# Routing the first batch in four parts instead of two, with one load and the first expert block moved in the order of issue

## The chip, the cores and the metric

The kernel runs on one core of a Trainium2 chip. The metric is the device time of one execution in microseconds (us). The engines are TensorE (PE, matmuls; PEld is its weight load), VectorE (DVE), ScalarE (ACT), GpSimd (POOL) and SyncE (SP), which here only issues DMAs. Each engine works through its own instructions in order; they wait for each other by semaphores.

## What is computed

The reference takes x of shape 8 x 2496 x 256 in float32, replaces it by the real part of its two-dimensional Fourier transform, and sends the 19968 rows through a mixture of 8 experts, each row through one:

```
X = np.fft.fft(np.fft.fft(x, axis=1), axis=2).real      # 8 x 2496 x 256
x = X.reshape(19968, 256)
logits = x @ w_gate                                     # 19968 x 8
expert_idx = np.argmax(logits, axis=1)
gate_w = softmax(logits)[arange, expert_idx]
for e in range(8):
    rows = expert_idx == e
    y[rows] = np.maximum(x[rows] @ w1[e], 0) @ w2[e]     # 256 -> 1024 -> 256
out = gate_w[:, None] * y
```

## The kernel before

A batch is one of the 8 sequences. Its way has these stages.

- **first(b)** (L325): loads x of the batch in three thirds (`load`, L284, 896 KB each, buffers of `xq`: three), folds each third on DVE (`fold`, L299; the folds' instructions are L306, L295, L296, L297), does the first step of the transform along the sequence on PE (`half1`, L311, tile `s`), copies it out on ACT (L321) and writes it to a scratch tensor Td in HBM (L342). For b of 1 and more it also issues the loads of batch b + 1.
- **regroup(b, h)** (L351): two DMAs on SP's queue that read Td back in another layout (tiles `t4`).
- **second(b)** (L361): in `group` (L374) the second step of the transform (tile `p2`, copied to `zz` at L379); then, for 2 halves of HW = 5 columns each, one column at a time: matmuls into `p3`, ACT's copies L405 and L408, DVE's pair of L410 that writes the rows, and ACT's `mirror` (L384). A column gives two slots of 128 rows, a half ten slots. PSUM tiles of all these come from one pool of three buffers.
- **route(b, h, rows, lg)** (L416): called once at the end of each half; 17 DVE instructions (L424 to L455), one exponential on ACT (L436) and eleven small matmuls (`rk`) that count rows by expert. They find each row's expert, gate and place in the sorted tensor Xs. `base`, the count so far, is handed from one call to the next. At its end the ten slots stand in the queue `waiting`.
- **send** (L462): takes one slot from `waiting` and issues its scatter on POOL, an indirect DMA of 128 rows to Xs (L236). For batch 0 the places are integers already; for later batches ACT and POOL convert them first (L468, L469).
- **plan(b, ...)** (L478): DVE instructions on one partition, which from `base` fix the blocks of rows that can be computed by now, and their expert. It has four yields; batch 0 has two plans, one for blocks of 256 rows (two blocks) and one for blocks of 128 rows (four).
- **experts(todo)** (L730): for each block SP reads the plan's table, loads the expert's weights (L546, L548, 1 MB each) and the block's rows (L536, L540) from Xs, `turn` transposes them on DVE (L584), then come the two matrix products (`ph`, `py`), and POOL scatters the result to the output. SP's load of the first rows waits for all scatters of its batch.

The order of all this on the engines is the order in which the Python program issues it: every stage is a generator, and a main loop (L997) takes a step of `experts` and, by a running account (`due`), so many steps of `side`, which holds the transforms and the routing of later batches. At the start (L967 on) `first(0)` runs through; then x of batch 1 and the two regroup issues of batch 0 go out; seven steps of `early` (which is `first(1)` and its regroup) are taken, and while `second(0)` runs, every second step of it is followed by one of `early`, and every step by a `send`. Then the expert generator starts: until the first plan's table is there it yields (L778), it fetches weights and rows, and then it yields nine more times (L784) before its first `turn`, so that steps of `side` come ahead of the first transposes in DVE's order and of the first `ph` in PE's. For b = 1, `side` weaves the plans of batch 0 with the rest of `early` and then the transforms of batch 1, one step of each by turns:

```
if b == 1:
    side = woven(chain(close(0), through(0)), chain(early, side))
```

The parts of the source that the change touches follow, with the line numbers that the profile uses.

Of the kernel before, what the change touches and what calls it, by code (L numbers as in the profile page):

```python
# [12 lines left out]
F32 = mybir.dt.float32  # L13
BF16 = mybir.dt.bfloat16
I32 = mybir.dt.int32
ALU = mybir.AluOpType
# [34 lines left out]
def bc(ap, axis, n):  # L51
    shape = list(ap.shape)
    shape.insert(axis, n)
    return ap[tuple([slice(None)] * axis + [None])].to_broadcast(shape)
# [127 lines left out]

TICKS = 32
LATE = 4
SHARE, EARLY, ROOM = 0.6, 0.7, 1.2
AHEAD = 12
WARM = 16
# [28 lines left out]
def kernel(ctx: ExitStack, tc, x, w_gate, w1, w2, out):  # L216
# [3 lines left out]
    def mm(o, lhsT, rhs, start=True, stop=True, **kw):  # L220
        nc.tensor.matmul(o, lhsT=lhsT, rhs=rhs, start=start, stop=stop, **kw)  # L221
# [62 lines left out]
    def load(b, q):  # L284

        if b < B:
            xq = xp.tile([NP, 8, D], F32, tag="xq", name="xq", bufs=3)
            row = (b * NQ + q) * NA
            nc.sync.dma_start(out=xq[:].rearrange("p j d -> p (j d)"), in_=x[row:row + NP])
            ahead[b, q] = xq[0:NA]  # L290
# [70 lines left out]
    def second(b):  # L361

        t4 = None

        def turn_last(h):

            nonlocal t4
            t4 = ahead.pop((b, "t4", h))
            n = min(HALF, NG - h * HALF)
            pr = pm_.tile([GP, HALF], F32, tag="m", name="pr")  # L370
            mm(pr[:, 0:n], con["rot"][:], t4[0:GP, 0:n, H])
            act.copy(t4[0:GP, 0:n, H], pr[:, 0:n])  # L372
# [13 lines left out]

        turn_last(0)
        yield
        group(0)
        yield  # L390
        group(1)
        yield
        for h in range(2):
            rows = sp.tile([128, NSL, W], F32, tag="rows", name="rows")
            lg = sp.tile([128, NSL, E], F32, tag="lg", name="lg")
            for i in range(HW):
                w, k = HW * h + i, 2 * i
                if w + 2 < NG:
                    group(w + 2)
                p3 = pm_.tile([128, 2 * NY + 2 * E + 1], F32, tag="m", name="p3")  # L400
                z = zz[:, :, 128 * w:128 * (w + 1)]
                mm(p3[:, 0:NY + 2 * E], z[:, 0], con["rd"][:, 0, 0:NY + 2 * E], True, False, skip_group_check=True)
                mm(p3[:, NY:], z[:, 1], con["rd"][:, 1], False, True, skip_group_check=True)
                zs = sp.tile([128, NY + 1], F32, tag="zs", name="zs")
                act.copy(zs[:], p3[:, NY + 2 * E:])  # L405
                if i:
                    mirror(rows, k - 2)
                act.copy(lg[:, k:k + 2], p3[:, NY:NY + 2 * E].rearrange("p (m e) -> p m e", m=2))  # L408
                for m, op in enumerate((ALU.add, ALU.subtract)):
                    vec.scalar_tensor_tensor(rows[:, k + m, 0:NY], p3[:, 0:NY], zs[:, 0:1], zs[:, 1:],  # L410
                                             op0=ALU.add, op1=op)
                yield
            mirror(rows, k)
            yield from route(b, h, rows, lg)

    def route(b, h, rows, lg):  # L416

        nonlocal base

        def small(name, *dims, dt=F32):  # L420
            return sp.tile([128, *dims], dt, tag=name, name=name)

        mx, eq, v = small("mx", NSL), small("eq", NSL, E), small("v", NSL)
        vec.reduce_max(mx[:], lg[:], axis=AX_X)  # L424
        vec.tensor_tensor(eq[:], lg[:], bc(mx[:], 2, E), op=ALU.is_equal)
        vec.tensor_tensor(eq[:], eq[:], bc(con["rev"][:], 1, NSL), op=ALU.mult)
        vec.reduce_max(v[:], eq[:], axis=AX_X)
        vec.tensor_tensor(v[:], v[:], con["good"][:, h], op=ALU.mult)
        oh = small("oh", NSL + 1, E, dt=BF16)
        vec.memset(oh[:, NSL], 0.0)  # L430
        vec.tensor_tensor(oh[:, 0:NSL], bc(con["rev"][:], 1, NSL), bc(v[:], 2, E), op=ALU.is_equal)
        yield

        su = small("su", NSL)
        vec.tensor_tensor(lg[:], lg[:], bc(mx[:], 2, E), op=ALU.subtract)
        act.activation(lg[:], lg[:], ACTF.Exp)  # L436
        vec.tensor_scalar(rows[:, :, D], con["row"][:, h], float(b * S), None, op0=ALU.add)
        yield

        rk = pm_.tile([128, NSL + 1, E], F32, tag="m", name="rk")  # L440
        mm(rk[:], tri[:], oh[:], True, False)
        for s in range(NSL):
            mm(rk[:, s + 1:], ones[:], bc(oh[:, s], 1, NSL - s), False, s == NSL - 1)
        vec.reduce_sum(su[:], lg[:], axis=AX_X)
        vec.tensor_scalar(su[:], su[:], 1e-9, None, op0=ALU.add)
        vec.reciprocal(rows[:, :, D + 1], su[:])
        yield

        pos, pf, pi = small("pos", NSL, E), small("pf", NSL), small("pi", NSL, dt=I32)
        vec.tensor_tensor(pos[:], rk[:, 0:NSL], bc(base[:], 1, NSL), op=ALU.add)  # L450
        vec.tensor_tensor(pos[:], pos[:], oh[:, 0:NSL], op=ALU.mult)
        vec.reduce_sum(pf[:], pos[:], axis=AX_X)
        vec.tensor_tensor(pf[:] if b else pi[:], pf[:], con["far"][:, h], op=ALU.add)
        nxt = cp.tile([128, E], F32, tag="base", name="base", bufs=2)
        vec.tensor_tensor(nxt[:], rk[:, NSL], base[:], op=ALU.add)  # L455
        base = nxt
        for s in range(NSL):
            waiting.append((b, pf[:, s:s + 1], pi[:, s:s + 1], rows[:, s]))

    waiting = deque()  # L460
# [269 lines left out]
    def experts(todo):  # L730
# [44 lines left out]
        for k, (b, size, last, at) in enumerate(todo):  # L775
            n, m = size // 128, BIG // size
            if not k:
                while todo[0][:3] not in tabs:  # L778
                    yield 0, False
                fetch_some(0, 1)  # L780
                while b not in whole:
                    yield 0, True
                fetch_some(0)
                for _ in range(9):  # L784
                    yield 0, False
                for xT in turn(b, size, xbs[0][0]):
                    pass
# [178 lines left out]
    todo = in_order()  # L966
    for _ in first(0):  # L967
        pass
    load(1, 0)
    load(1, 1)  # L970
    regroup(0, 0)
    regroup(0, 1)
    load(1, 2)
    nc.sync.dma_start(out=bt[:], in_=const_dram("blocks", cv))
    sent(unordered(nc.sync.dma_start(
        out=Xs[E * CAP:].rearrange("(k p) w -> p k w", k=BLK // 128), in_=bc(pad[:], 1, BLK // 128)), "xs"), 0)
# [20 lines left out]
    for b in range(1, B):  # L997

        done, due, room = 0, 0.0, 0.0
        side = chain(steps[b], islice(steps.get(b + 1, iter(())), AHEAD))  # L1000
        ticks = TICKS + AHEAD * (b == 1)
        if b == 1:
            side = woven(chain(close(0), through(0)), chain(early, side))
        blocks = [(size, k * size / BIG, halved(b - 1, size)) for size, k, _ in rounds()[b - 1]]
        total = sum(k * (15 if seven_ else 16) for _, k, seven_ in blocks)
        open_ = sum(k * (8 if seven_ else 16) for _, k, seven_ in blocks)
        while done < total:
            w, full = next(work)
# [72 lines left out]
```

## Time and profile before

| | us |
|---|---|
| eight executions: median (lowest to highest) | 1260.08 (1258.13 to 1261.27) |
| the profiled execution | 1256.42 |
| its span in the profile | 1254.6 |
| PE busy in the span | 1207.7 |
| DVE, POOL, ACT busy | 759.9, 447.3, 430.8 |
| mean clock granted to TensorE | 0.977 of full speed |

The page of the profile starts with each engine's busy time, its share of the span and its number of instructions. Below it the span is cut into 40 equal slices; a digit is the busy share of the slice in tenths, and the line PEclk is the clock that the throttle granted to TensorE, in tenths of full speed. A table of stretches has, for each stretch of time, its length, the busy time and the number of instructions of PE, PEld, DVE, ACT and POOL, then the granted clock, the share of time in which the DMA engines worked, and what they moved in GB/s. A line of the timeline has the start of a group of instructions, their busy time, the engine (SPq and ACTq are the issue of DMAs), the line of the kernel, the operation, what it writes and reads, and how many; in brackets stands how long the engine was idle just before, and what ended that.

### The profile page before, as it was taken

How to read it: one execution, taken by the hardware profiler on the slowest of the kernel's cores; microseconds unless marked ns; L12 is line 12 of the kernel's file. 1: busy time of each engine (PE TensorE's matmuls, PEld its weight loads, DVE VectorE, ACT ScalarE, POOL GpSimd, SP SyncE). 2: the span in 40 equal slices, each digit the busy share in tenths (PEclk: the TensorE clock that was granted, in tenths of full speed). 3: DMA queues.
4: the chain of work that ended last, by engine and by line, in shares of the span. 5: the costliest groups of instructions: out<-in, count | busy, mean ns of one | idle time of the engine just before them, and what ended most of it. 6: DMA issues, size and time to landing. Idle time of an engine off the chain costs nothing.

```text
span 1254.6 us, 22295 instructions
## 1 busy us (share of the span) xinstructions
PE 1207.7 (96%) x7289; PEld 1076.6 (86%) x7289; DVE 759.9 (61%) x1804; ACT 430.8 (34%) x1167; POOL 447.3 (36%) x527
## 2 busy tenths in 40 slices
PE   6759999999999999999999999999999999999997
PEld 4648988777788899888988899889999999999996
DVE  4546334333456788566865578686888884444663
ACT  1424333333244333434243433432333332222222
POOL 0245437064117421471226613472364241111112
PEclk6879999999999999999999999999999999999998
DMA  8859899873649434673336435453347238888887
GB/s 239 270 191 342 308 314 307 227 238 120 146 159 264 140 124 146 197 227 112 102 129 210 136 103 167 133 173 101 110 135 196 103 106 284 281 283 284 280 292 284
DMA packets 163216, 249.79 MB, mean 199 GB/s; under 512 B 118601, under 2 KB 130227, under 8 KB 143516
## 3 DMA queue, kind: packets, MB, share of 16 engines
q1 hardware_dynamic: 146327, 203.28, 51.7%
q0 software_dynamic: 15888, 42.14, 9.2%
q10 hardware_dynamic: 885, 2.94, 0.7%
q8 instruction: 59, 0.97, 0.3%
q14 instruction: 57, 0.47, 0.1%
HBM read 194.91 MB, written 54.83 MB: 199 GB/s over the span
## 4 chain that ended last, share of the span: by engine, by line
PE 82%; DVE 10%; DMA 3%; ACT 2%; issue 2%; POOL 0%; SPq 0%; POOLq 0%; DVEq 0%; ACTq 0%
PE py L221 25%; PE ph L221 13%; PE a L221 11%; PE c L221 9%; PE b L221 6%; PE p L221 6%; PE d L221 5%; PE e L221 4%; PE s L221 3%; DMA xq<-in_x_dram 1%; DVE xT L584 1%; DMA Td<-t 1%; DVE y L684 1%; DVE hT L636 1%; DVE hT L639 1%
## 5 line engine op out<-in xcount | busy, mean ns | idle before, releaser
L236 POOL DMA_INDIRECT out_dram<-y,ro x163 | 161.2, 989 | 625.6 <-ACT y L680 301.5
L221 PE MATMUL py<-w_sb,hT 128*128 128x256 f32 x1504 | 339.5, 380 | 0.0
L221 PEld LDWEIGHTS py<-w_sb,hT 128*128 128x128 f32 x1504 | 281.7, 190 | 36.5 <-issue 1.0
L236 POOL DMA_INDIRECT Xs<-rows,pi x160 | 162.4, 1015 | 110.0 <-DVE rows L410 54.8
L221 PE MATMUL ph<-xT,w_sb 128*128 128x128 f32 (+2 forms) x992 | 170.9, 328 | 11.1 <-DVE xT L584 11.0
L221 PEld LDWEIGHTS ph<-xT,w_sb 128*128 128x128 f32 x992 | 136.3, 193 | 35.1 <-issue 16.7
L410 DVE SCALAR_TENSOR_TENSOR rows<-p,zs 128x129 f32<-128x129 f32 x160 | 48.8, 348 | 128.6 <-ACT lg L408 124.6
L221 PE MATMUL a<-xT,w_sb 128*128 128x256 f32 (+1 forms) x512 | 117.8, 357 | 0.0
L838 DVE TENSOR_SCALAR hT<-ph 128x512 f32<-128x512 f32 x43 | 29.7, 691 | 123.7 <-PE ph L221 63.6
L587 ACT ACTIVATE xT<-xT 128x256 f32<-128x256 f32 (+1 forms) x94 | 36.5, 388 | 180.0 <-DVE xT L584 141.6
L221 PEld LDWEIGHTS a<-xT,w_sb 128*128 128x128 f32 x512 | 88.7, 191 | 9.7 <-DVE xT L584 0.2
L892 ACT ACTIVATE y<-py,xb 128x256 f32<-128x256 f32 x94 | 44.5, 473 | 151.5 <-PE py L221 150.4
L636 DVE TENSOR_TENSOR hT<-hT,b 128x512 f32<-128x512 f32 x57 | 39.2, 688 | 74.8 <-PE b L221 49.3
L646 ACT ACTIVATE hT<-a 128x512 f32<-128x512 f32 x57 | 34.0, 597 | 134.2 <-PE a L221 131.1
L221 PE MATMUL s<-xq,w 104*112 104x256 f32 (+2 forms) x208 | 62.6, 425 | 13.4 <-DVE xq L297 10.9
L469 POOL CAST pi<-due 128x1 int32<-128x1 f32 x140 | 45.1, 322 | 65.2 <-ACT due L468 65.2
L221 PE MATMUL a<-w_sb,hT 128*128 128x128 f32 x528 | 66.0, 276 | 0.0
L221 PEld LDWEIGHTS a<-w_sb,hT 128*128 128x128 f32 x528 | 63.1, 192 | 0.7
L221 PEld LDWEIGHTS p<-table,t 120*128 120x128 f32 x352 | 53.0, 200 | 10.7 <-ACT t L372 2.8
L221 PE MATMUL c<-xT,ws 128*128 128x256 f32 (+1 forms) x256 | 60.3, 363 | 1.0 <-DVE hT L642 0.2
L584 DVE STREAM_TRANSPOSE xT<-xb 128x512 f32<-128x512 f32 (+1 forms) x91 | 56.3, 631 | 7.6 <-DMA xb<-Xs 7.6
L221 PE MATMUL b<-xs,ws 128*128 128x256 f32 (+1 forms) x256 | 58.8, 357 | 0.0
(149 smaller groups left out, 2052.8 us busy)
## 6 DMA issues: line engine op xcount, KB each, us to landing
w_sb<-in_moe_w_dram SPq DMA_DIRECT2D x132, 1024.0 KB
xq<-in_x_dram SPq DMA_DIRECT2D x24, 896.0 KB
xb<-Xs SPq DMA_DIRECT2D x112, 128.0 KB
Td<-t SPq DMA_DIRECT2D x18, 448.0 KB
t<-Td SPq DMA_DIRECT2D x8, 768.0 KB
t<-Td SPq DMA_DIRECT2D x8, 640.0 KB
xb<-Xs SPq DMA_DIRECT2D x52, 64.0 KB
xb<-Xs SPq DMA_DIRECT2D x88, 32.0 KB
```

The lines of the kernel that those rows point to most:

```text
L221: nc.tensor.matmul(o, lhsT=lhsT, rhs=rhs, start=start, stop=stop, **kw)
L236: return unordered(pool.indirect_dma_start(out=dst, out_offset=bass.IndirectOffsetOnAxis(ap=idx, axis=0), in_=rows, in_offset=None, bounds ...
L410: vec.scalar_tensor_tensor(rows[:, k + m, 0:NY], p3[:, 0:NY], zs[:, 0:1], zs[:, 1:], op0=ALU.add, op1=op)
L469: pool.tensor_copy(idx, due[:])
L584: vec.transpose(free(xT[:], 256 * h, [32, n // 32], [BIG, 2], [1, 32]), free(xb, 512 * h, [64, n // 32], [1, 2], [2, 32]))
L587: act.activation(odd, odd, ACTF.Copy, scale=-1.0)
L636: vec.tensor_tensor(h12, h11, b[:], op=add)
L639: vec.tensor_tensor(h21, h12, d[:], op=add)
L646: act.activation(h11, a[:], ACTF.Relu)
L684: vec.tensor_tensor(o, o, p[:], op=add)
L838: vec.tensor_scalar(o, ph[:], 0.0, None, op0=ALU.max)
L892: act.activation(y[:, i % 2], py[:], ACTF.Copy, scale=meta[:, i, 1:2])
```

## The change

It has four parts.

1. `second` calls `route` for batch 0 four times, behind the second, fifth, eighth and tenth column (PARTS: two and three columns in the first half, three and two in the second), with the slots of those columns alone: 4, 6, 6 and 4 slots. Batches 1 to 7 keep two calls. `route` takes a slice of slots; its small tiles are cut to it, and the tiles of places `pf` and `pi` get four buffers. The memset of `oh` moves one instruction ahead, and the mirror of a part's last column is issued at its end.
2. The load of batch 1's third third of x is issued on SP ahead of the two regroup issues of batch 0 instead of behind them.
3. The expert generator yields twelve times and not nine ahead of the first turn.
4. For b = 1 five steps of the plans of batch 0 are taken alone, before the rest of the plans is woven with the transforms of batch 1.

In the order of the built program, four groups of `rk` matmuls (5, 7, 7 and 5) take the place of two of eleven. The first plan and half of the second stand on DVE ahead of the fold of batch 2's first third, where they were mixed with it. The two last `half1` of batch 1 stand behind the second and third column of batch 0 and no longer behind the fourth and fifth. Ahead of the first `ph` on PE stand three columns of batch 1, where there were four. The diff, cut to its core:

```
+PARTS = ((2, 3), (3, 2))
...
         for h in range(2):
...
+            ends = list(np.cumsum(PARTS[h] if not b else (HW,)))
+            lo = 0
             for i in range(HW):
...
-                if i:
+                if i and i not in ends:
                     mirror(rows, k - 2)
...
                 yield
-            mirror(rows, k)
-            yield from route(b, h, rows, lg)
+                if i + 1 in ends:
+                    mirror(rows, k)
+                    yield from route(b, h, rows, lg, slice(lo, k + 2))
+                    lo = k + 2
 
-    def route(b, h, rows, lg):
+    def route(b, h, rows, lg, at):
...
+        n = at.stop - at.start
+        rows, lg = rows[:, at], lg[:, at]
+        mx, v, su = (small(name, NSL)[:, 0:n] for name in ("mx", "v", "su"))
+        eq, pos = (small(name, NSL, E)[:, 0:n] for name in ("eq", "pos"))
+        pf = sp.tile([128, NSL], F32, tag="pf", name="pf", bufs=4)[:, 0:n]
+        pi = sp.tile([128, NSL], I32, tag="pi", name="pi", bufs=4)[:, 0:n]
+        oh = small("oh", NSL + 1, E, dt=BF16)[:, 0:n + 1]
...
-        for s in range(NSL):
-            mm(rk[:, s + 1:], ones[:], bc(oh[:, s], 1, NSL - s), False, s == NSL - 1)
+        for s in range(n):
+            mm(rk[:, s + 1:], ones[:], bc(oh[:, s], 1, n - s), False, s == n - 1)
...
-        for s in range(NSL):
+        for s in range(n):
             waiting.append((b, pf[:, s:s + 1], pi[:, s:s + 1], rows[:, s]))
...
-                for _ in range(9):
+                for _ in range(12):
                     yield 0, False
                 for xT in turn(b, size, xbs[0][0]):
...
-    load(1, 0)
-    load(1, 1)
+    for q in range(NQ):
+        load(1, q)
     regroup(0, 0)
     regroup(0, 1)
-    load(1, 2)
...
         if b == 1:
-            side = woven(chain(close(0), through(0)), chain(early, side))
+            plans = close(0)
+            side = chain(islice(plans, 5), woven(chain(plans, through(0)), chain(early, side)))
```

More of the change, by code (lines that the diff above doesn't have):

```diff
@@ L421, in small @@
             return sp.tile([128, *dims], dt, tag=name, name=name)
[L423 to L429, printed above, removed]
@@ L430, in route @@
-        vec.memset(oh[:, NSL], 0.0)
-        vec.tensor_tensor(oh[:, 0:NSL], bc(con["rev"][:], 1, NSL), bc(v[:], 2, E), op=ALU.is_equal)
+        n = at.stop - at.start
[4 more added lines that the diff above has]
+        pi = sp.tile([128, NSL], I32, tag="pi", name="pi", bufs=4)[:, 0:n]
@@ L432, in route @@
+        oh = small("oh", NSL + 1, E, dt=BF16)[:, 0:n + 1]
+        vec.reduce_max(mx, lg, axis=AX_X)
+        vec.tensor_tensor(eq, lg, bc(mx, 2, E), op=ALU.is_equal)
+        vec.tensor_tensor(eq, eq, bc(con["rev"][:], 1, n), op=ALU.mult)
+        vec.reduce_max(v, eq, axis=AX_X)
+        vec.tensor_tensor(v, v, con["good"][:, h, at], op=ALU.mult)
+        vec.memset(oh[:, n], 0.0)
+        vec.tensor_tensor(oh[:, 0:n], bc(con["rev"][:], 1, n), bc(v, 2, E), op=ALU.is_equal)
         yield
-        su = small("su", NSL)
@@ L435, in route @@
-        vec.tensor_tensor(lg[:], lg[:], bc(mx[:], 2, E), op=ALU.subtract)
-        act.activation(lg[:], lg[:], ACTF.Exp)
-        vec.tensor_scalar(rows[:, :, D], con["row"][:, h], float(b * S), None, op0=ALU.add)
+        vec.tensor_tensor(lg, lg, bc(mx, 2, E), op=ALU.subtract)
+        act.activation(lg, lg, ACTF.Exp)
+        vec.tensor_scalar(rows[:, :, D], con["row"][:, h, at], float(b * S), None, op0=ALU.add)
         yield
-        rk = pm_.tile([128, NSL + 1, E], F32, tag="m", name="rk")
@@ L441, in route @@
-        mm(rk[:], tri[:], oh[:], True, False)
-        for s in range(NSL):
-            mm(rk[:, s + 1:], ones[:], bc(oh[:, s], 1, NSL - s), False, s == NSL - 1)
-        vec.reduce_sum(su[:], lg[:], axis=AX_X)
-        vec.tensor_scalar(su[:], su[:], 1e-9, None, op0=ALU.add)
-        vec.reciprocal(rows[:, :, D + 1], su[:])
-        yield
-        pos, pf, pi = small("pos", NSL, E), small("pf", NSL), small("pi", NSL, dt=I32)
-        vec.tensor_tensor(pos[:], rk[:, 0:NSL], bc(base[:], 1, NSL), op=ALU.add)
@@ L451, in route @@
-        vec.tensor_tensor(pos[:], pos[:], oh[:, 0:NSL], op=ALU.mult)
-        vec.reduce_sum(pf[:], pos[:], axis=AX_X)
-        vec.tensor_tensor(pf[:] if b else pi[:], pf[:], con["far"][:, h], op=ALU.add)
+        rk = pm_.tile([128, NSL + 1, E], F32, tag="m", name="rk")[:, 0:n + 1]
+        mm(rk, tri[:], oh, True, False)
+        for s in range(n):
+            mm(rk[:, s + 1:], ones[:], bc(oh[:, s], 1, n - s), False, s == n - 1)
+        vec.reduce_sum(su, lg, axis=AX_X)
+        vec.tensor_scalar(su, su, 1e-9, None, op0=ALU.add)
@@ L454, in route @@
+        vec.reciprocal(rows[:, :, D + 1], su)
+        yield
+        vec.tensor_tensor(pos, rk[:, 0:n], bc(base[:], 1, n), op=ALU.add)
+        vec.tensor_tensor(pos, pos, oh[:, 0:n], op=ALU.mult)
+        vec.reduce_sum(pf, pos, axis=AX_X)
+        vec.tensor_tensor(pf if b else pi, pf, con["far"][:, h, at], op=ALU.add)
         nxt = cp.tile([128, E], F32, tag="base", name="base", bufs=2)
-        vec.tensor_tensor(nxt[:], rk[:, NSL], base[:], op=ALU.add)
+        vec.tensor_tensor(nxt[:], rk[:, n], base[:], op=ALU.add)
```

## The prediction, made before the changed kernel was run

> **What bounds the kernel now.** I read the page first, then the stretches, then the timeline of the first 100 us; every number below is from these views of the kernel before, except where I say "worked out".
>
> On the page the engine line of TensorE (PE) comes first, then its row of slices:
>
> ```profile
> PE 1207.7 (96%) x7289; PEld 1076.6 (86%) x7289; DVE 759.9 (61%) x1804; ACT 430.8 (34%) x1167; POOL 447.3 (36%) x527
> PE   6759999999999999999999999999999999999997
> PEclk6879999999999999999999999999999999999998
> ```
>
> PE is full from the fourth slice to the last. So the end is: the moment at which PE becomes full, plus the PE work that is left then. The table of stretches gives that moment:
>
> ```profile
> 62.00:76.50 14.50, 10.98 (x52) 9.17 (x52) 12.20 (x56) 5.00 (x18) 11.45 (x11) 0.73 0.74 261
> 76.50:87.50 11.00, 0.00 (x0) 0.00 (x0) 2.71 (x8) 0.66 (x4) 3.89 (x4) 0.67 0.37 104
> 87.50:110.00 22.50, 21.65 (x123) 19.02 (x124) 9.78 (x36) 10.05 (x37) 4.85 (x9) 0.93 0.92 305
> ```
>
> From 76.5 to 87.5 PE does nothing; after it PE is busy 21.65 of 22.5 us, and so on to the end. Who ends the hole is in the timeline:
>
> ```profile
> 53.24 1.11 POOL L236 DMA_INDIRECT Xs<-rows,pi  x1 [52.79 <-DVE rows L410]
> 54.65 0.97 POOL L236 DMA_INDIRECT Xs<-rows,pi  x1 [0.30 <-issue]
> ...
> 63.65 1.89 POOL L236 DMA_INDIRECT Xs<-rows,pi  x1 [0.30 <-issue]
> ...
> 80.33 0.97 POOL L236 DMA_INDIRECT Xs<-rows,pi  x1 [0.30 <-issue]
> 82.93 1.92 SPq L536 DMA_DIRECT2D xb<-Xs  x4
> 86.74 0.71 DVE L584 STREAM_TRANSPOSE xT<-xb 128x512 f32<-128x512 f32 x1 [7.56 <-DMA xb<-Xs]
> 87.50 3.42 PE L221 MATMUL ph<-xT,w_sb 128*128 128x256 f32 x8 [11.04 <-DVE xT L584]
> ```
>
> The first block needs all 20 scatters of batch 0. POOL issues them in one unbroken row, 53.24 to 80.33, 1.28 us apart; then come landing, fetch, transpose. So the path is: routing of the first half, 20 scatters, turn. The change acts on its head.
>
> **Part by part** (lines are those of before; columns of batch 0 are counted from 0).
>
> *The load moved forward* (L973). One SP issue passes the two regroup issues; no instruction is added. Before, it was issued at 30.16 and VectorE (DVE) stood on it until 39.10; the fold behind it ended just as the first L410 could start, 41.85, though lg was there at 41.19. Gain at most 0.7. Loss: its 0.92 MB now run beside the third write of Td0 (25.71 to 29.05), for which regroup waits. DMA moved 356, 260 and 18 GB/s in the stretches 24-26, 26-28, 28-30; the empty last stretch takes some 0.65 MB, the rest costs 0.8 us at 350 GB/s; with no room at all 2.7 us. I take 0 (0.7 against 0.8), bounds -0.7 and +2.7.
>
> *Four routes for two.* A ten-slot route takes DVE from 48.75 (L424) to 52.39 (L455), 3.64 us, 17 instructions that wait for each other. A narrower one has the same 17; its wide ones fall from 0.24 (128x80) towards 0.17 (the 1x32 row), so some 3.3. Two more routes are 6.6 us of DVE ahead of everything later on DVE. On PE the extra rk matmuls (11 take 0.47) are nothing; on ACT two 0.27 exps. The wait added: ACT's exp stands before the copies of the next column, so ACT idles in each route.
> - Column 1's L410 ends at 43.6. Route 1: 43.5 to 46.9. POOL started 1.1 after L453 (52.14 to 53.24), so here at 47.7, 5.5 earlier; four scatters, free at 52.9.
> - Columns 2 to 4 took 44.15 to 48.83, 4.7 us, with the two half1 copies between them. Behind route 1 (ACT and PE run ahead at most by the three buffers of PSUM) they end at 51.9. Route 2: to 55.2, its scatters ready at 56.0. **POOL stands still from 52.9 to 56.0.**
> - Columns 5 to 7 and route 3: 61.7, ready 62.6, ahead of POOL (56.0 + 6 x 1.28 = 63.7). Columns 8, 9 and route 4: 66.7, ready 67.6, ahead of 71.4.
> - Last scatter: 56.0 + 15 x 1.28 = 75.2. Four scatters of before are longer than 0.97 (63.65: 1.89, 65.84: 1.26, 71.24: 1.64, 78.30: 1.72), each beside a fold of x (L306, L295, L296) on DVE. Two folds fall on the last scatters again: I add the first three excesses, 1.9. **77.1 instead of 80.33**; bounds 75.2 and 77.8.
>
> Here a page speaks against the change. The Trainium skill, SBUF — State Buffer, section "SBUF: two separate sides", says that VectorE and GpSimd share a port pair as a lock and that the loser is blocked for the whole instruction. By that a fold's 1.21 + 0.67 + 0.67 could hold scatters for 5.1 us in two folds, the last scatter would start at 80.3 and the sum below would come out near 1262. The trace agrees in part only: the scatter at 67.41 took 0.97 beside the fold at 67.53.
>
> *From the last scatter to the turn.* 80.33 to 87.50 is 7.17. The last scatter landed in 2.35; the median of the 20 is 4.6. Before, the weights (2 MB) were issued at 68.17 and DMA was full until 78, so the last scatter found it empty. Now the plan ends later: route 4 at 66.7, then 20 plan instructions, 1.41 + 0.43 + 1.36 in their three groups, at 70.0; weights until some 80. I add 0.55 of the possible 2.25, as they are nearly through: first ph at 77.1 + 7.17 + 0.55 = **84.8** (84.3 to 86.5).
>
> *Plans first, twelve steps.* In the built program five plan steps now stand ahead of the folds of batch 2, and one column fewer of batch 1 stands ahead of the first ph. On DVE, worked out: ten more plan instructions to 72.0, fold to 75.0, rest of the plan and second fold to 78.9, then three L410 pairs behind matmuls that start on the half clock (s at 66.42: 2.02 for four): the third ends at 83.65. The transpose stands behind it, so ph could start at 84.4. This hides behind the scatters by 0.4 us only; each later us of DVE would then count in full.
>
> *The sum at the turn.* Turn: 84.8 - 87.50 = -2.7. The column deferred behind it (p, pr, p) is 0.94 + 0.13 at full clock: +1.1. **The clock:** the granted clock fell to 0.5 at 59.75 and 80.25, 3.2 and 3.8 us after the last matmul, and came back at 91, so the first ph took 3.42 instead of 1.89 (91.71). With PE at work until 82.3 by the DVE count and the turn at 84.8 the gap is 2.5: -1.5 (0 if cold). Behind the turn DVE has the small fold (L295 to L306, 1.6 us) that was done before it; rk may wait: +0.3 (0 to 1.6). Weights, x and Td2 move with the turn: 0. Sum -2.7 + 1.1 - 1.5 + 0.3 = **-2.8**.
>
> The profiled execution took 1256.42 (span 1254.6 and 1.8 around it): 1253.6. The median of the eight runs is 1260.08, 3.66 above; I carry the difference over: **1257.3 us**. Measurement tells about 0.2%, 2.5 us, from no change.
>
> **Rivals.**
> - *Full gain* (0.25). Routes overlap better, two more cost 4.6 and not 6.6, and POOL hardly stands still: scatters from 47.7 back to back end at 47.7 + 19 x 1.28 + 1.9 = 73.9; DVE is then the bound at 82.4. -5.1 + 1.1 - 1.5 = -5.5: 1254.6. For it: 0.54 us of DVE idle per column. Against: ACT is held by the exp.
> - *The gain is eaten at the turn* (0.15). The last scatter lands in 4.6, ph at 86.5, PE has gone cold: -1.0 + 1.1 + 0.3 = +0.4: 1260.5. For it: the weights come later. Against: DMA is empty at 78 to 80.
> - *The clock falls in the routes* (0.15), the slower case. PE's gaps in the routes are 2.4 to 2.9 by my times; one of 3.4 halves the clock, and the thin work of columns does not lift it (62 to 70 stayed at 0.5 for 3.5 us of steady work). Then p and p take 1.75 and not 0.95 in seven columns: DVE is 5.6 late, ph at 90.0. +2.5 + 1.1 + 0.3 = +3.9: 1264. It decides from a gap of 3.4 us, and makes it slower once the transpose starts after 86.
> - That the change doesn't do what it says is excluded by the built order: four rk groups, the scatters of the first four slots behind the first.
>
> **How the numbers follow.** The forecast has 0.45. With errors of 0.5 to 1 us in several terms, two thirds of it lie beyond 2.5 us: faster 0.30 + 0.25 = 0.55; same 0.15 + 0.15 = 0.30; slower 0.15. The range takes in the full gain and the eaten one with the bounds of the load and of the deferred fold around them, and leaves out most of the clock case: 1253.8 to 1261.6.
>
> **What would show it.** Right: first scatter near 47.7; a hole on POOL of some 3 us after the fourth; last scatter near 77; weights issued near 70.5; first ph near 85 with eight matmuls in 1.9. Wrong: no hole (full gain), a granted clock of 0.5 between 50 and 66 (clock case), a first L410 after 43 (the load), a transpose that waits for DVE's own queue and not for xb (DVE has become the bound).

## The result, and the profile after

| | before | after |
|---|---|---|
| executions: median (lowest to highest), us | 1259.95 (1257.02 to 1262.36) | 1266.42 (1263.66 to 1269.43) |
| the profiled execution, us | 1256.42 | 1264.91 |
| its span, us | 1254.6 | 1263.1 |
| VectorE (DVE) busy, us | 759.9 | 765.1 |

The changed kernel is slower: 1.0054 times the time before, 95% interval 1.0045 to 1.0063. The forecast was 1257.3, the upper end of the range 1261.6.

One caution for all that follows. The profiled execution of before lies 3.5 us below the median of its kernel; those of the other kernels on the quicker chips (see the experiments) lie within 3 us of theirs, on either side. So a difference between two traces tells where time goes, and the ratios tell how much.

On the page of after, the slices of TensorE (PE) and its granted clock:

```profile
PE   5659999999999999999999999999999999999997
...
PEclk9769999999999999999999999999999999999998
```

PE is full from the fourth slice on, as before. Most of the loss is made ahead of that. The stretches, with the columns of the table of before:

```profile
62.00:76.50 14.50, 6.00 (x36) 5.26 (x34) 10.55 (x64) 4.09 (x16) 10.72 (x12) 0.61 0.64 205
76.50:87.50 11.00, 6.74 (x28) 6.00 (x28) 8.57 (x29) 2.96 (x10) 4.15 (x3) 0.58 0.73 237
87.50:110.00 22.50, 18.19 (x99) 15.48 (x100) 11.11 (x39) 8.21 (x30) 1.43 (x4) 0.92 0.79 245
```

Before, PE worked 10.98 us in the first of these, nothing in the second and 21.65 in the third. Now work has spread into the hole (6.74 between 76.5 and 87.5), at a clock of 0.58, and the third stretch is no longer full. The timeline of POOL shows the 20 scatters:

```profile
51.51 1.11 POOL L237 DMA_INDIRECT Xs<-rows,pi  x1 [51.06 <-ACT lg L411]
...
59.71 0.97 POOL L237 DMA_INDIRECT Xs<-rows,pi  x1 [3.27 <-DVE rows L413]
...
77.77 2.07 POOL L237 DMA_INDIRECT Xs<-rows,pi  x1 [0.30 <-issue]
80.14 1.12 POOL L237 DMA_INDIRECT Xs<-rows,pi  x1 [0.30 <-issue]
```

and that of SP's queue the weights of the first block, then its rows, which wait for the last scatter's landing:

```profile
76.44 0.37 SPq L554 DMA_DIRECT2D w_sb<-in_moe_w_dram  x1
...
87.44 1.92 SPq L544 DMA_DIRECT2D xb<-Xs  x4
```

The first scatter starts 1.7 us sooner than before (forecast 5.5), the hole behind the fourth is there as forecast (3.27 us), and the last scatter starts at 80.14, where it stood before. Then 7.30 us pass until the rows can be fetched; before it was 2.60. The first ph follows at 92.10 instead of 87.50.

### The profile page after: what moved, and what is told of

It is laid out like the page before. It is cut to its first block, busy times and chain, and to the rows that moved or that the text cites. A ratio compares the mean times of both kernels' runs of the same rounds, so it can differ in the third digit from the quotient of the medians.

```text
span 1263.1 us, 22338 instructions
## 1 busy us (share of the span) xinstructions
PE 1211.0 (96%) x7291; PEld 1079.2 (85%) x7291; DVE 765.1 (61%) x1838; ACT 431.8 (34%) x1169; POOL 445.1 (35%) x527
## 4 chain that ended last, share of the span: by engine, by line
PE 83%; DVE 9%; DMA 3%; ACT 2%; issue 2%; POOL 1%; SPq 0%; POOLq 0%; DVEq 0%; ACTq 0%
PE py L222 24%; PE ph L222 12%; PE a L222 11%; PE c L222 10%; PE p L222 6%; PE b L222 6%; PE d L222 5%; PE e L222 4%; PE s L222 3%; DMA Td<-t 1%; DVE xT L592 1%; DVE y L692 1%; DMA xq<-in_x_dram 1%; DMA Xs<-rows,pi 1%; DVE hT L644 0%
## 5 line engine op out<-in xcount | busy, mean ns | idle before, releaser
L237 POOL DMA_INDIRECT Xs<-rows,pi x160 | 159.7, 998 | 111.5 <-ACT lg L411 51.8
L413 DVE SCALAR_TENSOR_TENSOR rows<-p,zs 128x129 f32<-128x129 f32 x160 | 48.8, 348 | 143.5 <-ACT lg L411 138.8
L222 PEld LDWEIGHTS s<-xq,w 104*112 104x112 f32 x208 | 38.1, 203 | 29.7 <-issue 11.2
L222 PE MATMUL p<-table,t 120*128 120x120 f32 (+1 forms) x352 | 58.7, 293 | 2.0 <-ACT t L373 2.0
```

The source lines that it names most:

```text
L237: return unordered(pool.indirect_dma_start(out=dst, out_offset=bass.IndirectOffsetOnAxis(ap=idx, axis=0), in_=rows, in_offset=None, bounds ...
```

## The experiments

Eighteen runs of twelve kernels stand in five groups, each group beside before on one chip. In three groups before took 1259.1 to 1260.1, as in the first result; two fell on other chips, where before took 1273.3 and 1274.6. There ACT and DVE stand still in three to five places, for 0.4 to 6.4 us. One of ACT's lines in load_back:

```profile
68.81 0.27 ACT L408 COPY zs<-p 128x130 f32<-128x130 f32 x1 [3.95 <-remote]
```

The bracket says that ACT was idle for 3.95 us and that nothing on this core released it. No trace of the quicker chips has such a line, and I did not find the cause. The intervals of those two groups are about twice as wide, so the verdicts rest on the others; the labels are marked "slower chip".

| label | what it is | ratio to before | interval |
|---|---|---|---|
| after_again | the changed kernel | 1.0044 | 1.0026 to 1.0062 |
| load_back_again | after, load put back | 1.0022 | 1.0010 to 1.0033 |
| load_alone_again | before, load moved | 1.0011 | 0.9999 to 1.0023 |
| w2_behind | after, load put back, second weight matrix behind the rows | 1.0006 | 0.9993 to 1.0019 |
| order_alone_third | before, twelve steps, five plan steps alone | 1.0019 | 1.0009 to 1.0030 |
| routes_alone_again | before, four routes | 1.0006 | 0.9997 to 1.0015 |
| routes_w2_12_again | four routes, twelve steps, second matrix behind | 1.0015 | 1.0005 to 1.0024 |
| w_behind | the same, both matrices behind | 1.0017 | 1.0008 to 1.0026 |
| w_behind_9 | the same with nine steps | 1.0002 | 0.9992 to 1.0011 |
| three_routes | before, three routes | 1.0014 | 1.0004 to 1.0023 |
| load_back | slower chip | 0.9991 | 0.9972 to 1.0011 |
| load_alone | slower chip | 1.0012 | 0.9985 to 1.0040 |
| routes_alone | slower chip | 1.0021 | 1.0001 to 1.0042 |
| order_alone | slower chip | 1.0016 | 0.9995 to 1.0038 |
| order_alone_again | slower chip | 1.0007 | 0.9988 to 1.0026 |
| before_w2_behind | slower chip | 0.9989 | 0.9971 to 1.0007 |
| routes_w2 | slower chip, four routes, second matrix behind | 0.9991 | 0.9972 to 1.0009 |
| routes_w2_12 | slower chip, as routes_w2_12_again | 0.9975 | 0.9960 to 0.9991 |

My theory after the result (theory 1): the moved load delays a write to Td and all that hangs on it. The rival (theory 2): the loss is made at the turn, by the order there and by weights that stand beside the last scatter's landing.

### The load

```diff
-    for q in range(NQ):
-        load(1, q)
+    load(1, 0)
+    load(1, 1)
     regroup(0, 0)
     regroup(0, 1)
+    load(1, 2)
```

load_back is after with this edit; load_alone is before with its reverse. First on a slower chip:

> The changed kernel with the load of batch 1's last third back behind the two regroup issues; the rest of the change stays. Theory 1 (the load): beside it the third write of Td0 landed at 32.95 and not at 29.05, and everything behind regroup is 3.9 us late. Then regroup is issued near 29, the first scatter comes near 47.7, the turn near 88, and the time falls by some 4 us from 1266.4 to about 1262.5. Theory 2 (the order at the turn: plans first, weights beside the last scatters, which lands 7.05 us after its issue where it was 2.35): the late regroup is absorbed by the waits behind it, and the time stays within 1 us of 1266.4.

> The kernel before with nothing changed but the load in front of the regroup issues. Theory 1: regroup near 33, first scatter near 57, turn near 91.4, 1264 us. Theory 2: no more than 1 us above 1260.

Measured: 0.9991 and 1.0012, neither of which tells one theory from the other there. The marks in the trace were as theory 1 has them: regroup issued at 29.49 with the load put back, at 32.56 with the load alone moved. Then again, beside after itself, on a quicker chip:

> The changed kernel itself, unaltered, as the standard for the three runs beside it. Both theories expect a ratio of 1.0045 to 1.0063 against before, as in the first result, and on this chip or any other the same marks in the trace: regroup of batch 0 issued about 33.0, last scatter begun about 80.1 and landed about 7 us later, first rows issued about 87.4.

> The changed kernel with the last third of batch 1's x put back behind the two regroup issues, once more, beside the changed kernel itself. Theory 1 (the moved load delays the write to the scratch tensor, and with it everything up to the turn): regroup issued at 29.0 to 29.5 instead of 33.0, first scatter about 48, routes done about 3.5 us sooner than in the changed kernel, ratio against before 1.000 to 1.003, which is 0.002 to 0.005 below the changed kernel. Theory 2 (the loss is made at the turn, where 2 MB of weights stand in front of the last scatter's packets): the first rows are issued no sooner than 87 us, and the ratio stays at 1.004 or more.

> The kernel before with nothing but the load moved ahead of the regroup issues. Theory 1: regroup issued about 3.5 us later, first scatter 2 to 3.5 us later than in before, last scatter up to 3 us later (POOL's 20 scatters are bound there by their own 1.28 us each), ratio 1.002 to 1.004. Theory 2: ratio within 1.001, since the order at the turn is that of before.

Measured: 1.0044, 1.0022, 1.0011. (In after_again the last scatter began at 81.81 and the rows were issued at 88.88, 1.7 and 1.5 us later than expected; that goes with the clock, below.) In the trace of after, the issues of the load, of the third write to Td (ACT's queue) and of the two regroup reads:

```profile
24.90 0.31 SPq L290 DMA_DIRECT2D xq<-in_x_dram  x1
...
26.80 0.31 ACTq L343 DMA_DIRECT2D Td<-t  x1
...
32.95 0.99 SPq L355 DMA_DIRECT2D t<-Td  x2
```

The same write and reads in load_back_again:

```profile
26.26 0.31 ACTq L343 DMA_DIRECT2D Td<-t  x1
...
29.92 0.99 SPq L355 DMA_DIRECT2D t<-Td  x2
```

From the issue of the write to that of the reads, which wait for its landing, it is 6.15 us with the load beside it and 3.66 without (3.34 before; 6.65 in load_alone_again). The DMA engines in after while the write is under way (PE busy, clock, DMA share, GB/s):

```profile
28.00:30.00 2.00, 0.13 (x1) 0.50 1.02 268
30.00:32.00 2.00, 2.00 (x5) 0.50 0.75 272
32.00:34.00 2.00, 1.63 (x4) 0.50 0.01 4
```

They are full until 30 and empty from 32: the write does not land until the load has nearly gone through. So the load costs 0.0022 of after's 0.0044 when taken out of it (the intervals overlap a little; that of the first result, from 1.0045, lies above), and 0.0011 when put into before (its interval reaches down to 0.9999), where POOL has no hole: its last scatter starts at 83.47 there instead of 80.33. Theory 1 is right on the mechanism, and load_back_again lies in its range; for load_alone_again it expected 0.002 to 0.004. Half of after's loss is left without the load.

### The weights beside the last scatter

The first block's weights are two matrices of 1 MB. w2_behind is load_back with the second fetched behind the block's rows (`True` makes fetch_weights put it off); before_w2_behind is before with that alone; w_behind has both behind, with the load put back and plans woven as in before, and twelve steps:

```diff
-                fetch_some(0, 1)
+                got.append(fetch_weights(tabs[b, size, last], at, True))
                 while b not in whole:
                     yield 0, True
+                xbs.append(fetch_rows(b, size, tabs[b, size, last], at))
+                w2_sb, tab, i = held.pop()
+                fetch_w2(w2_sb, nc.sync.value_load(tab[:, 1, i:i + 1], min_val=0, max_val=E - 1))
```

> The changed kernel with the load put back, and with the second weight matrix of the very first expert block (1 MB) fetched behind that block's rows instead of ahead of them; the first matrix (1 MB) stays ahead. Theory 2, and theory 1 with a part for the landing: only 1 MB stands beside the last scatter, which lands 2.5 to 4.5 us after its start instead of about 7; the first rows are issued 2 to 3 us sooner than in the version with only the load put back, and the ratio is 0.001 to 0.003 lower than its. If the slow landing is not from the weights: landing 6 us or more, rows no sooner, ratio within 0.001 of its.

> The kernel before with only the first block's second weight matrix fetched behind its rows. There its weights were issued at 68.2 us, 12 us ahead of the last scatter, so nothing stands beside that scatter's landing. Both theories expect no gain: first rows issued within 0.3 us of 82.9, ratio 0.999 to 1.001. A ratio under 0.998 would say that this fetch costs time by itself, wherever it stands.

> As routes_w2_12_again, but both weight matrices of the first block fetched behind its rows, so that none stands beside the last scatter. Theory A: that scatter lands 2.3 to 3 us after its start, as in before, the first rows are issued 1 to 2 us sooner than with one matrix ahead, but the first matrix then lands some 4 to 5 us behind the rows, so that the first ph is not sooner; ratio within 0.001 of routes_w2_12_again. If the landing stays at 4 us or more with nothing beside it, the weights are not its cause.

Measured: 1.0006 against 1.0022 for load_back_again in the same group; 0.9989, no difference, for before_w2_behind; 1.0017 for w_behind, as expected within 0.001 of routes_w2_12_again (1.0015). The DMA engines in after around the last scatter's landing (columns as above):

```profile
82.00:84.00 2.00, 2.00 (x10) 0.50 1.02 425
84.00:86.00 2.00, 2.00 (x11) 0.59 0.63 246
86.00:88.00 2.00, 1.69 (x12) 1.00 0.01 4
```

They move the weights at up to 425 GB/s until some 85, and from 86 hardly anything. SP's queue in w2_behind, where one matrix goes ahead:

```profile
72.61 0.37 SPq L556 DMA_DIRECT2D w_sb<-in_moe_w_dram  x1
80.47 1.93 SPq L544 DMA_DIRECT2D xb<-Xs  x4
```

Its last scatter starts at 76.33, 4.14 us ahead of the rows. And w_behind, POOL's last scatter, then SP's queue:

```profile
77.23 0.97 POOL L237 DMA_INDIRECT Xs<-rows,pi  x1 [0.31 <-issue]
```

```profile
79.86 1.96 SPq L544 DMA_DIRECT2D xb<-Xs  x4
...
83.22 0.36 SPq L554 DMA_DIRECT2D w_sb<-in_moe_w_dram  x1
```

2.63 us, as before. All the traces of the quicker chips fall in three classes:

| weights beside the last scatter | from its start to the rows' issue, us |
|---|---|
| none (before, load_alone_again, order_alone_third, w_behind, w_behind_9) | 2.60, 2.62, 2.72, 2.63, 2.64 |
| 1 MB (w2_behind, routes_w2_12_again) | 4.14, 4.68 |
| 2 MB issued 1.8 to 3.7 us ahead (after, after_again, load_back_again, routes_alone_again) | 7.30, 7.07, 7.18, 7.14 |

(three_routes issued 2 MB 7.6 us ahead, and took 4.11.) So this is shown: the weights of the first block, which four routes make late, hold the last scatter's landing by 4.5 us. By the medians the second matrix costs 0.0016 (the intervals overlap). It is no more since DVE is next: in w2_behind the rows were issued 5 us sooner than in load_back_again (3.0 by the landing; 0.7 by an earlier regroup and 1.3 by a shorter hole on POOL, 3.28 and not 4.56, which goes with the clock, below), but the transpose, at 85.83, stood behind a pair of L413 that began at 85.30.

### The order at the turn

order_alone is before with parts 3 and 4 of the change; it ran three times.

```diff
-                for _ in range(9):
+                for _ in range(12):
...
-            side = woven(chain(close(0), through(0)), chain(early, side))
+            plans = close(0)
+            side = chain(islice(plans, 5), woven(chain(plans, through(0)), chain(early, side)))
```

> The kernel before with twelve steps and five plan steps first; two routes, load as before. Theory 1: within 1 us of 1260. Theory 2: the plan's table is ready earlier, but one column less stands ahead of the turn and folds stand on the last scatters: 1263 us or above, with the last scatter landing 5 us or more after its issue.

> The kernel before with nothing but twelve steps ahead of the first turn and five plan steps taken alone. Theory A (these two parts keep TensorE idle, since the fold of batch 2's first third and so the half1 behind it wait for the plan, and they defer a column behind the first product): PE idle by some 4 us more than in before between 60 and 87 us, first ph within 1 us of 87.5, ratio 1.001 to 1.003. Theory B (the two parts are worth what they were costed at or gain, and the loss is that of the four routes): ratio 0.998 to 1.000.

> The kernel before with twelve steps and five plan steps alone. Theory A: the half1 of batch 2 waits for the fold behind the plan, PE's gap ahead of it grows from 1.9 to 6 us or more, ratio 1.001 to 1.003. Theory B: ratio 0.998 to 1.000, and no gap of over 4 us appears.

Measured: 1.0016 and 1.0007 on slower chips, which settle nothing, and 1.0019 (1.0009 to 1.0030) on a quicker one. Theory 2 had the wrong reason (the scatter landed in 2.72, the weights were issued sooner, at 66.92) and the right sign. PE in order_alone_third:

```profile
70.98 2.02 PE L221 MATMUL s<-xq,w 104*112 104x256 f32 x4 [5.62 <-issue]
...
86.84 3.78 PE L221 MATMUL ph<-xT,w_sb 128*128 128x256 f32 x8 [8.62 <-DVE xT L584]
...
122.81 1.99 PE L221 MATMUL ph<-xT,w_sb 128*128 128x256 f32 x8 [1.23 <-DVE hT L838]
```

The fold that the s matmuls need stands behind the plan on DVE, so PE waits 5.62 for it (1.94 before). The bracket names no releaser, but the fold's last instruction (L297) starts on DVE at 70.72. The first ph is 0.66 sooner than before all the same, and still the kernel is slower. A view across kernels shows where that comes back: how much later than in before the scatter of the output starts that is at a given time in before.

| at, in before | 107.2 | 136.4 | 139.2 | 152.9 | 293.8 |
|---|---|---|---|---|---|
| after | 5.19 | 5.19 | 6.65 | 7.99 | 7.99 |
| load_back_again | 3.17 | 3.18 | 4.64 | 5.99 | 5.99 |
| w2_behind | -1.98 | -1.99 | -0.54 | 0.83 | 0.83 |
| order_alone_third | 0.76 | 0.77 | 2.24 | 3.57 | 3.58 |
| load_alone_again | 3.31 | 3.30 | 3.30 | 3.30 | 3.30 |
| routes_alone_again | 3.70 | 3.73 | 3.75 | 3.72 | 3.73 |
| w_behind_9 | 1.22 | 1.21 | 1.21 | 1.21 | 1.21 |

Every kernel with twelve steps and plans first loses 2.8 us in two steps of 1.3 to 1.5 between 136 and 153; every kernel with nine and woven plans loses none there. By size the steps fit the column put off (1.1) and the stall of ph on hT at 122.81 (1.23), which stands in after at 127.23 and in none of the nine-step traces. With twelve steps and woven plans (w_behind and routes_w2_12_again below) the stall is not there, and the output at 152.9 is later than that at 136.4 by 1.7 and not by 2.8. That fits, but the order of the outputs' delays differs there as well, so the two are not separated.

Is it the steps or the plans? Four routes with the second matrix behind, and plans woven (the edit to w2_behind below), once with nine steps (routes_w2) and twice with twelve:

```diff
-            plans = close(0)
-            side = chain(islice(plans, 5), woven(chain(plans, through(0)), chain(early, side)))
+            side = woven(chain(close(0), through(0)), chain(early, side))
```

> Four routes and four buffers of places alone (load, nine steps and woven plans as in before), with the first block's second weight matrix fetched behind its rows. Theory A: without the load's delay, the weights beside the landing and the order at the turn, the four routes show their own worth: last scatter begun 76 to 77, first rows issued 80 to 82, first ph 85 to 87 with four columns of batch 1 ahead of it, ratio 0.997 to 0.999. Theory B: the sparse columns at half clock and 36 more DVE instructions in front of the turn keep it at 1.000 to 1.002.

> The same with twelve steps ahead of the first turn and not nine, plans still woven. Against the earlier run with twelve steps and five plan steps alone (ratio 1.0006) it shows what those plan steps alone cost. Theory A: the half1 of batch 2 no longer waits behind the plan, PE's 7.3 us of idle time ahead of it shrink below 4, ratio 0.998 to 1.000. Theory B: within 0.0005 of 1.0006.

> Four routes, load as before, second weight matrix of the first block behind its rows, twelve steps, plans woven: once more. Theory A (the four routes gain when the load, the weights and the plan steps are out of the way): ratio 0.997 to 0.9995, that is 0.001 or more below the same with five plan steps alone (1.0006). Theory B (they don't): 1.0 to 1.002.

> As w_behind (four routes, both weight matrices of the first block behind its rows, woven plans), with nine steps ahead of the first turn as in before. Theory B (the order on VectorE held the transpose): route and fold of batch 1 stand behind the transpose again, which starts at 85 to 86.5 and not 90; first ph at 86.5 to 88, held by the first matrix, which is issued about 83; ratio 0.998 to 1.0. Theory A: the ratio stays above 1.0005, since the columns ahead of the turn come later by the two routes.

Measured: 0.9991, and 0.9975 (0.9960 to 0.9991) on the slower chip. The second looked like a version that beats before, and was not: on the quicker chip it gave 1.0015. Theory A fell there, and why that order helps on the slower chips stays open. DVE in w_behind, which has the same twelve steps and woven plans:

```profile
87.02 0.23 DVE L435 TENSOR_REDUCE mx<-lg 128x10 f32<-128x80 f32 x1
...
88.47 0.68 DVE L296 TENSOR_TENSOR xq<-xq 104x508 f32<-104x508 f32 x1
...
89.97 0.70 DVE L592 STREAM_TRANSPOSE xT<-xb 128x512 f32<-128x512 f32 x1
```

Twelve steps without the plans ahead of them reach into batch 1's route (from 87.02, L435) and the next fold (88.47). They stand in front of the transpose (L592), whose rows were issued from 79.86. With nine steps, in w_behind_9, the transpose starts at 86.10, and it is now the first matrix for which ph waits:

```profile
87.88 3.75 PE L222 MATMUL ph<-xT,w_sb 128*128 128x256 f32 x8 [4.42 <-DMA w_sb<-in_moe_w_dram]
```

Measured: 1.0002 (0.9992 to 1.0011), the best of the versions with four routes on the quicker chips, and equal to before. The marks are those of theory B, the ratio lies just above its range.

### The routes

routes_alone is after with the load put back, nine steps and woven plans; three_routes has also PARTS = ((3, 2), (5,)).

> The kernel before with four routes for batch 0 and the four buffers of places; load, steps and plans as before. By the working of the forecast: first scatter near 47.7, a stand of POOL of 3 us after the fourth, last scatter near 77; the plan is mixed with the folds again. Theory 1: turn near 85 to 86, 1257 to 1259 us. Theory 2: the same or a little better, since the order at the turn is the old one. If neither: the two added routes cost as much as they bring, 1260 or above.

> The kernel before with the four routes and four buffers of places alone. Theory A: the weights are issued some 5 us later than in before (the last route ends later) and stand beside the last scatter, which lands 5 to 7 us after its start: the scatters' lead is eaten there, ratio 1.000 to 1.002. Theory B (the routes by themselves gain what they save on POOL): last scatter 76 to 77, landed within 3 us, ratio 0.997 to 0.998.

> Batch 0 routed in three parts (three, two and five columns), load, nine steps and woven plans as in before. Theory A (each added route costs its 3.2 us, and some more at half clock, on the chain that ends in the plan): last route ends about 66 and not 70 to 71, plan 1 about 72, weights issued about 72.5 and landed ahead of the last scatter, which begins at 78 to 79 and lands within 4 us; first rows 81 to 82.5, first ph 85.5 to 87, ratio 0.998 to 0.9995. Theory B (the routes' number doesn't matter, the steps at the turn do): ratio within 0.0005 of 1.0006.

Measured: 1.0021 on the slower chip, where less was expected, and 1.0006 on the quicker one, as theory A had it, but for the weights, which came 9 us later than in before and not 5: issued at 77.43, last scatter at 79.21, landing 7.14. three_routes gave 1.0014, where 0.998 to 0.9995 was expected. The weights did land sooner (4.11), but its last route ended at 68.46 and not at 66, and POOL stood still for 5.48 us ahead of the last ten scatters:

```profile
69.31 0.97 POOL L237 DMA_INDIRECT Xs<-rows,pi  x1 [5.48 <-ACT zz L380]
```

What I had left out is the clock. PE's wait for the one-hots of the first route, in w2_behind and then in load_back_again:

```profile
45.01 0.18 PE L222 MATMUL rk<-oh,tri 128*128 128x40 bf16 x1 [1.68 <-DVE oh L441]
```

```profile
45.76 0.18 PE L222 MATMUL rk<-oh,tri 128*128 128x40 bf16 x1 [1.71 <-DVE oh L441]
```

Up to there both kernels issue the same instructions, and the waits are alike; but the clock stayed at 1.00 behind the first and was halved behind the second. In each trace the changes of the granted clock lie whole multiples of 3.41 us apart, and where these moments fall in the program differs from run to run. Here are the stretches between such moments (PE busy, clock, DMA share, GB/s), in w2_behind:

```profile
40.81:44.23 3.42, 2.52 (x16) 1.00 1.02 296
44.23:47.64 3.41, 2.54 (x22) 1.00 0.93 296
47.64:51.05 3.41, 2.85 (x22) 1.00 0.64 137
```

and in load_back_again:

```profile
42.42:45.83 3.41, 1.16 (x7) 1.00 1.02 279
45.83:49.24 3.41, 3.41 (x18) 0.50 0.61 228
```

In w2_behind the wait (43.33 to 45.01) is divided between two stretches, and PE is busy for 2.5 us of each. In load_back_again it lies in one stretch, whose busy time is 1.16, and the clock of the next is 0.50. All twelve traces of the quicker chips, cut like this and without their last 15 us, say the same: a stretch at full clock was followed by one at half clock 47 times, always with PE busy for at most 1.88 us of it, and by another at full clock 4101 times, always with 1.94 or more. (In the last 15 us it fell once in each trace, behind 1.53 to 2.59; that stays open.) So the length of a gap does not decide by itself. The first route's gaps are 1.51 to 1.72 us in all twelve, and behind six of them the clock fell; a gap of 2.05 us ahead of w2_behind's first ph (86.58) left it at 1.00, with 2.44 and 2.02 busy in the two stretches that share it. Behind the gaps of 2.56 to 2.86 of the second to fourth route it fell, or stayed down, every time. Nor does the change itself choose: after and after_again are the same kernel, and behind the first route the clock stayed up in after and fell in after_again, where POOL's hole was 4.60 us and the last scatter began at 81.81, 1.7 later. Columns then come further apart. Two L413 pairs of the third part in after:

```profile
61.33 0.61 DVE L413 SCALAR_TENSOR_TENSOR rows<-p,zs 128x129 f32<-128x129 f32 x2 [1.80 <-ACT lg L411]
62.93 0.61 DVE L413 SCALAR_TENSOR_TENSOR rows<-p,zs 128x129 f32<-128x129 f32 x2 [0.99 <-ACT lg L411]
```

They are 1.60 us apart, and the first of them 2.41 behind the pair at 58.92; before, at full clock, the pairs from 54.43 to 57.88 came every 1.15.

## Why the prediction was wrong

In the profiled execution the forecast was 1253.6 and the measurement 1264.91, 11.3 us more (by the medians, 1257.3 and 1266.42, it is 9.1). First ph was forecast at 84.8 and came at 92.10, which is 7.3 of it: 3.0 at the start of the last scatter (80.14 and not 77.1), 4.15 at its landing, 0.1 behind that. Three terms made this.

- **"I take 0" for the load** (bounds -0.7 and +2.7). The first L413 came at 45.75 instead of 41.85. The working put the write and the load on the queues as if the load could use empty time behind the write. It took the write's own time, and the write landed with the load: regroup 3.9 us later than in before, with the DMA engines at 268 to 272 GB/s between 28 and 32 and not at the 350 of the working. Worth 0.0011 to 0.0022, that is 1.4 to 2.8 us.
- **The routes' ends, 46.9, 55.2, 61.7 and 66.7.** Without the load's delay and with the clock up through the first route (w2_behind) they were at 46.66, 55.01, 62.86, 68.50 (L463): the route's 3.3 us and the columns between were right, until the clock fell behind the second. In routes_alone_again, where it fell behind the first, they were 48.03, 57.69, 65.54, 71.19. The case of the clock was on the list, with 0.15, and was said to decide "from a gap of 3.4 us"; the gaps of 2.4 to 2.9 that I had worked out were enough. The Trainium skill's page "TensorE: Matmul & The Clock Gate", section "Part 1: The HAM clock gate", gives an idle window of about 3.4 us, and calls it free-running. The traces agree with a free-running window, of 3.41 us, but it did not have to be idle: the clock fell behind windows in which PE was busy for up to 1.88 us. So "from a gap of 3.4 us" was the wrong measure, and whether the first route lost the clock was luck.
- **"I add 0.55 of the possible 2.25"** for the landing. It was 4.70 (7.30 against 2.60). Two things failed. The weights were issued at 76.44 and not at 70.5, since the last route and with it the plan ended some 5.8 us later than worked out, so they were not "nearly through"; and the bound of 2.25 came from the median of the 20 scatters (4.6), where the longest of them (7.7) was the row to take. The rival "the gain is eaten at the turn" named this mechanism and priced it at half.

The last scatter itself, 77.1 with the hole at 52.9 to 56.0, was well forecast for a clock that holds through the first route. Without the load it was then 76.33 in w2_behind (hole from 52.60 to 55.88) and 76.96 in w_behind_9; with the clock down there it was 77.23 to 79.21 (w_behind, routes_w2_12_again, load_back_again, routes_alone_again). With the load it was 80.14. Only one fold stood beside the last two scatters of after, from 77.78 on, and not two; they took 2.07 and 1.12, which is 1.25 over 0.97 each, where the prediction had added 1.9. By the lock of the Trainium skill's page "SBUF — State Buffer", section "SBUF: two separate sides", as the prediction used it, one fold could have held them for 2.55, half of the 5.1 that it worked out.

Of the other 4 us: the cold first ph (3.46 and not 1.89; its gap was 3.73) is 1.5, forecast as a gain. "Plans first, twelve steps" was priced at +1.1 for the column and +0.3 for the fold; the two steps in the table of outputs are 2.8, 1.4 more. That leaves about 1.1 us unassigned. The working missed that the plans ahead of the fold take away the s matmuls that filled PE's time between 66 and 76.

Taken one at a time, the load costs 0.0011, the order 0.0019 and the routes 0.0006: 0.0036 together, against 0.0044 and 0.0054 for the whole, which the intervals do not tell apart. No part gains by itself. What four routes save on POOL, 1.1 to 4.0 us at the last scatter once the load is put back, goes into later weights and a later plan; put those out of the way (w_behind_9), and the first ph waits for the first weight matrix instead (87.88, 0.4 later than before).

Open: the stall of ph on hT and the column put off were not separated; nine steps, woven plans and one matrix behind were run on a slower chip only (0.9991); what halts the slower chips; and why routes_w2_12 gained there.

## What to carry to other kernels

When work in front of a hand-over is cut finer to start it sooner, look at what the finer cut makes late: here a table of counts needed the last part, and the 2 MB of weights that hang on the table moved from 12 us ahead of the last small write to the very place where that write had to land. A transfer that is moved ahead of a dependent read is not free while any write that the read waits for is still on its way. And a thin stage has to be costed by how long PE is busy in each 3.41 us: here, below some 1.9 us, the next 3.41 us ran at half clock, and which gaps cause that depends in part on luck.

## What the runs showed of the hardware that I had not expected

- The last scatter of 128 rows landed, by the issue of the read that waits for it, 2.6 to 2.7 us after its start with nothing beside it, 4.1 to 4.7 beside 1 MB and 7.1 to 7.3 beside 2 MB of loads issued 1.8 to 3.7 us ahead of it on another queue. In after it came in only when the loads had gone through; 2 MB issued 7.6 us ahead left 4.1.
- A write of 448 KB to HBM took 3.1 to 3.7 us from its issue to the issue of the read that waits for it, and 6.2 to 6.7 beside a load of 896 KB that was issued 0.6 to 1.9 us ahead of it.
- The granted clock of TensorE changed only at moments whole multiples of 3.41 us apart. It fell behind stretches in which PE was busy for 1.88 us or less (47 of them) and stayed up behind those with 1.94 or more (4101), in twelve traces without an exception outside their last 15 us.
